# Three late score tiles exponentiated by VectorE, and the last chunk's tables made in two halves

## The chip, the cores and the metric

The kernel runs on one NeuronCore of a Trainium2 chip. The metric is the device time of one execution in microseconds (us), as the median of several. TensorE (PE in the profile) does matmuls, ScalarE (ACT) activations, VectorE (DVE) elementwise work, GpSimd (POOL) and SyncE (SP) mostly issue transfers here.

## The reference

Two mixers read the same input x (2048 positions, 448 channels, bf16) and are blended by a gate per position.

```
g = sigmoid((x * gate_w).sum(-1))
a = attention(x): 16 heads of 28 channels, one shared key/value head
    p = softmax(q k^T / sqrt(28)) ; o = p v ; a = o wo
b = state space convolution along positions:
    K[d,l] = Re( sum_n C[d,n] exp(dt[d] A[d,n] l) dt[d] B[d,n] ),  n < 256
    y[:,d] = causal convolution of x[:,d] with K[:,d] (by FFT of twice the length) ; b = y + x * Dskip
out = g * a + (1 - g) * b
```

The attention has 16 x 2048 x 2048 scores, all of which need an exponential. The convolution kernel K has 448 x 2048 entries, each a sum over 256 complex modes.

## The kernel before

**Attention.** The scores are cut into 1024 tiles of 128 keys by 512 queries. Sixteen blocks of queries and heads (index `i`) each hold 64 tiles: 16 key tiles for four heads. Tiles are worked in sets of three and two alternately (`sets` in `main`). For each set TensorE writes the scores to PSUM banks 0 to 4 (`qk`, lines 483, 1504 and 1498), ScalarE takes the exponential of the whole set in one instruction (line 1546) into `expT`, a ring of 15 tiles in SBUF, and two sets later TensorE multiplies four tiles at a time by the values (`pv`, lines 1570 and 1564) into the bank `psB`. The softmax sum is a column of ones among the values. When a block of 64 is done, `norm` copies `psB` out, sends the sums through DRAM and scales the result (lines 1237 to 1249); `outp` multiplies by the output matrix. The last block is finished in three parts (`PARTS`, `scaled`, `last`), so that little is left behind the last exponential. `early` adds two of the four head groups' products for the last block beforehand; `HELD` names the convolution steps behind which that is put.

**Convolution.** The channels are worked in 14 chunks of 32 (`c`). For each, `masters` squares the modes' step repeatedly and writes bf16 copies to `mbf` (line 1015), and `tables` (lines 1038 to 1088) builds on VectorE the powers from which K is made: five levels of complex products, each twice as wide as the one before it (lines 1052 and 1067), a real decay table in `tmp` (1071, 1075), and its products (1081, 1085, 1088). Two small copies on POOL start a chunk's tables. `kgen` turns them into K by matmuls (line 1111), in two halves of 16 channels with 32 matmuls each, stages them in `kstg` (1123), and stores them to DRAM (`KP`). `tload` reads them back as shifted tiles in `T` or `U`, and `conv` multiplies these with the input (1178), scales by 1 - g (1188), folds the result (1199) and adds it to the output tile `O` (1208). Chunk c has convolutions 2c and 2c + 1; the last chunk, `LASTQ` = 13, has 26 and 27. All tables of a chunk are made before any of its `kgen` matmuls.

**Order.** Every operation is entered with its reads, writes, an estimated length and a priority. `Prog.schedule` then plays all engines forward by these estimates and writes down a fixed order for each; dependences between engines become semaphore waits. Where TensorE would be idle, it puts in a filler matmul (line 1453). Its constants (`PUSH`, `SLACK`, `LATE` among others) say how much later than estimated a transfer or an operand may be taken to arrive. `HOLDC` holds two convolution steps of chunk 12 behind the last `kgen`. At run time each engine works through its own list strictly in order.

**Buffers of the change.** `xT` holds the input for the query projections, `qM` a wide copy of the queries, used by those score tiles that run on the full array (line 1504); late sets (`ROWS` = 320 and on) don't use it. Line 192 issues every transfer.

Of the kernel before, what the change touches and what calls it, by code (L numbers as in the profile page):

```python
# [7 lines left out]
ALU = mybir.AluOpType  # L8
# [4 lines left out]
P = 128  # L13
# [8 lines left out]
W2 = 2 * D  # L22
# [26 lines left out]
HELD = ((27, 3), (27, 9), (27, 15), (27, 21))  # L49
# [11 lines left out]
HOLDC = (((24, 8), 7), ((25, 0), 7))  # L61
# [19 lines left out]
        120, 165, 138, 131, 139, 152, 140, 167, 164, 154, 188, 168, 189, 169, 193, 190, 191, 195, 1739, 197,  # L81
        1740, 198, 200, 1741, 202
# [36 lines left out]
class Prog:  # L119
# [13 lines left out]
    PUSH, PUSHES = 1.1, 100.0  # L133
    POOL = (7, 5)
    SLACK = {"pe": 500.0, "dve": 300.0}
    FAR = 2500.0
    LAZY = {1.15: 200.0, 1.55: 200.0, 1.58: 200.0, 1.6: 200.0}
    LATE = 1000.0
# [362 lines left out]
class Kernel:  # L501
# [442 lines left out]
    def qproj(self, i):  # L944
# [30 lines left out]
        if True:  # L975
            pg.dma([(self.qM.v(32 * h, 32, s * XQ + 512 * h, [[1, 512]]), self.qT.v(32 * h, 32, 512 * s, [[1, 512]]))
                    for h in range(4)], (128, 1024), f"qm{s}", rd=[("q", s)], wr=[("qM", s)], pr=0, eng="pool", extra=4500)

    def masters(self, b):
# [13 lines left out]
        for k in range(11):  # L993
# [7 lines left out]
            if k == 5:  # L1001
# [13 lines left out]
            pg.op("dve", lambda e, off=off: e.tensor_copy(mbf.v(0, P, off, [[128, 2], [MC, nb], [1, 64]]),  # L1015
                                                          self.seedz.v(0, P, o, [[W2, 2], [64, nb], [1, 64]])),
                  el(2 * n, 1.92), rd=[kr, ki] + first + done, wr=[("mb", k)], pr=pr)

    def tables(self, c):
# [24 lines left out]
        for lv in range(5):  # L1044
# [25 lines left out]
        rk = [("tmp", 0), ("tmp", 1)]  # L1070
        vo(lambda e: e.tensor_copy(rho.v(0, P, 62, [[64, 32], [1, 2]]), mq(0)), 64,
           [("mq", 0)], rk)
        for lv in range(5):
            w = 1 << lv
            vo(lambda e, w=w, lv=lv: e.tensor_tensor(rho.v(0, P, (32 - 2 * w) * 2, [[64, 32], [2, w], [1, 2]]),  # L1075
                                                     rho.v(0, P, (32 - w) * 2, [[64, 32], [2, w], [1, 2]]),
                                                     self.mq.v(0, P, lv * W2 + 64 * c, [[2, 32], [0, w], [1, 2]]), ALU.mult), w * 64,
               [("mq", lv)] + rk, rk)
# [11 lines left out]

    def kgen(self, c):
# [4 lines left out]
        keys = self.tabkeys  # L1096
        ko = self.kstg
        rs = ko.rs
        for q in range(2):
            G = self.grp()  # L1100
            for k in range(4):
                m = 4 * q + k

                def mm(e, m=m, k=k, G=G):
                    for comp in range(2):
                        for half in range(2):
                            cg = half * 16 + 2 * m
                            for u in range(2):
                                fo = lo + comp * PL + (32 + cg) * 64 + u
                                mo = FM + comp * FP + cg * 64 + u  # L1110
                                r = e.matmul(
                                    G.v(64 * u, 64, 128 * k, [[1, 128]]),
                                    tab.v(0, P, lo + comp * PL + cg * 64 + u, [[2, 64]]),
                                    tab.v(0, P, fo, [[64, 2], [mo - fo, 2], [2, 32]]),
                                    start=(comp == 0 and half == 0), stop=(comp == 1 and half == 1),
                                    tile_position=(0, 64 * u), skip_group_check=True)
                    return r
                o = pg.op("pe", mm, 245, mode="h", ni=16, rd=keys,
# [298 lines left out]
    def main(self):  # L1417
        pg = self.pg
        kT, qT, expT, vaug = self.kT, self.qT, self.expT, self.vaug
        NTL = 1024  # L1420
        sets, t = [], 0
        while t < NTL:
            n = min(2 if len(sets) % 2 else 3, NTL - t)
            sets.append(list(range(t, t + n)))
            t += n
# [14 lines left out]
        for ts in sets:  # L1440
            bs, es = sorted(t % 5 for t in ts), sorted(t % RING for t in ts)
            for t, b, x in zip(ts, bs, es):
                bank[t], ring[t] = b, x
        spread = lambda x, n: [[512 * (x[1] - x[0]), n], [1, 512]] if n > 1 else [[1, 512]]
# [13 lines left out]
        def qk(s):  # L1458
# [4 lines left out]
            def row(e):  # L1463
                r = None
                if ts[-1] >= NLAST:
# [41 lines left out]
            if s < 8 or len(ts) == 3 or s >= 14 and (ts[0] % 64 < NEWQ or s >= ROWS):  # L1507
# [7 lines left out]
                if ts[-1] < NLAST and ts[0] > 64:  # L1515
                    o.pre = pre
# [23 lines left out]
            es = [ring[t] for t in ts]  # L1540
            ew = [("e", x) for x in es]
            for t in ts:
                x = ring[t] if t <= RING else 0
                ew += ["Wk"] if x == RING - 1 else ["Wv", "Wvg", "Wm"] if x == RING - 2 else self.xk(3) if 9 <= x < 13 else self.xk(2) if 5 <= x < 9 else []
            n = len(ts)
            o = pg.op("act", lambda e: e.activation(expT.v(0, P, 512 * es[0], spread(es, n)),  # L1546
                                                self.psS.v(0, P, 512 * bs[0], spread(bs, n)),
                                                AF.Exp, scale=SQ), 63.5 + 426.5 * n, rd=bk, wr=ew, pr=0)
            self.lastexp = o.i
            if s == GATEOUT:  # L1550
                self.gw.deps[o.i] = 1

        def pv(v):
# [4 lines left out]
            def mm(e, ts=ts):  # L1558
                if ts[0] >= NLAST:
                    q0, nq = PARTS[declast(ts[0])[0]]  # L1560
                    for x in range(512 // nq):
                        for t in ts:
                            p, kt, h = declast(t)
                            r = e.matmul(self.psB.v(32 * h, 32, q0, [[1, nq]]), vaug.v(0, P, 32 * (kt + x), [[1, 32]]),
                                         expT.v(0, P, 512 * ring[t] + nq * x, [[1, nq]]),
                                         start=(kt + x == 0), stop=(kt + x == 15), tile_position=(0, 32 * h), skip_group_check=True)
                    return r
                for t in ts:
                    i, kt, h = dec(t)
                    r = e.matmul(self.psB.v(32 * h, 32, 0, [[1, 512]]), vaug.v(0, P, 32 * kt, [[1, 32]]),  # L1570
                                 expT.v(0, P, 512 * ring[t], [[1, 512]]),
# [7 lines left out]
            o = pg.op("pe", mm, 230, rd=["va"] + [("e", ring[t]) for t in ts], wr=[("b", 6)], pr=0.5 if v < NTL // 4 - 2 else -1, mode="c", ni=8)  # L1579
# [6 lines left out]
            if end:  # L1586
# [4 lines left out]
                self.copied = o.i  # L1591
        nv = 0
        self.lastpv = None
        self.pvs, self.qks = [], []
        for s in range(len(sets)):
            qk(s)
            last = sets[s][-1]
            if s >= 2:
                while nv < NTL // 4 and 4 * nv + 3 <= sets[s - 2][-1]:
                    pv(nv)  # L1600
# [12 lines left out]
        for b, (c0, nb) in enumerate(BLOCKS):  # L1613
            self.masters(b)
            for c in range(c0, c0 + nb):
                self.tables(c)
# [59 lines left out]
```

## Time and profile before

| | |
|---|---|
| median of 3 runs | 497.94 us (495.91 to 501.37) |
| profiled execution | 499.41 us |
| its span | 497.5 us |
| TensorE busy | 468.4 us, 94% of the span |
| VectorE busy | 456.5 us, 92% |
| ScalarE busy | 482.7 us, 97% |
| exponentials (line 1546) | 464.8 us in 410 instructions |
| mean granted TensorE clock | 0.993 |

Durations are of one profiled execution. "Busy" merges overlapping instructions; the length of one instruction can overlap the next one's start on the same engine, so the distance from start to start is what an instruction occupies. Idle time ahead of an instruction is printed with what ended it; "issue" means that the profile shows nothing that it waited for. A matmul group's "x18" counts instructions. The granted clock is TensorE's share of full speed.

### The profile page before, as it was taken

How to read it: one execution, taken by the hardware profiler on the slowest of the kernel's cores; microseconds unless marked ns; L12 is line 12 of the kernel's file. 1: busy time of each engine (PE TensorE's matmuls, PEld its weight loads, DVE VectorE, ACT ScalarE, POOL GpSimd, SP SyncE). 2: the span in 40 equal slices, each digit the busy share in tenths (PEclk: the TensorE clock that was granted, in tenths of full speed). 3: DMA queues.
4: the chain of work that ended last, by engine and by line, in shares of the span. 5: the costliest groups of instructions: out<-in, count | busy, mean ns of one | idle time of the engine just before them, and what ended most of it. 6: DMA issues, size and time to landing. Idle time of an engine off the chain costs nothing.

```text
span 497.5 us, 17528 instructions
## 1 busy us (share of the span) xinstructions
PE 468.4 (94%) x7685; PEld 219.8 (44%) x7752; DVE 456.5 (92%) x850; ACT 482.7 (97%) x434; POOL 213.9 (43%) x390
## 2 busy tenths in 40 slices
PE   8999999999999999999999999999999999989997
PEld 6433233452542534454443335444435444444554
DVE  6999999999999999999999999999999999993325
ACT  6999999999999999999999999999999999998995
POOL 8402135334143434749339355872747342521110
PEclk9999999999999999999999999999999999997999
DMA  8970015818408654896914919886494949492842
GB/s 244 278 155 13 3 33 147 276 28 267 134 18 260 196 156 117 239 267 177 289 30 95 324 25 255 243 217 172 114 241 108 290 84 356 141 327 89 241 153 71
DMA packets 91912, 85.45 MB, mean 172 GB/s; under 512 B 25242, under 2 KB 86860, under 8 KB 91836
## 3 DMA queue, kind: packets, MB, share of 16 engines
q1 hardware_dynamic: 80938, 72.54, 50.1%
q0 software_dynamic: 10624, 11.70, 10.1%
q8 instruction: 61, 1.00, 0.8%
q14 instruction: 15, 0.12, 0.1%
q10 hardware_dynamic: 274, 0.08, 0.1%
HBM read 76.36 MB, written 5.23 MB: 164 GB/s over the span
## 4 chain that ended last, share of the span: by engine, by line
ACT 41%; DVE 30%; PE 20%; DMA 4%; SPq 2%; issue 1%; ACTq 0%
ACT expT L1546 41%; DVE tab L1052 10%; DVE tab L1067 5%; PE psS L483 3%; PE psB L1570 3%; DVE tab L1081 2%; PE psX L1178 2%; PE psS L1178 2%; DMA T<-in_B_A_re_dram 2%; SPq L192 2%; PE psS L1504 2%; DVE tmp L1075 2%; DMA T<-KP_scratch 1%; DVE kstg L1123 1%; DVE msq L995 1%
## 5 line engine op out<-in xcount | busy, mean ns | idle before, releaser
L1546 ACT ACTIVATE expT<-psS 128x1536 bf16<-128x1536 f32 (+1 forms) x410 | 464.8, 1331 | 5.9 <-PE psS L483 4.7
L1052 DVE TENSOR_TENSOR tab<-tab,mbf 128x256 bf16<-128x256 bf16 (+4 forms) x140 | 138.7, 996 | 0.0
L483 PE MATMUL psS<-qT,kT 32*128 32x512 bf16 x703 | 100.8, 383 | 7.6 <-ACT expT L1546 3.6
L1570 PE MATMUL psB<-expT,vaug 128*32 128x512 bf16 x992 | 99.5, 391 | 0.9 <-DVE acc L1237 0.9
L192 POOL DMA_DIRECT2D KP_scratch<-kstg x104 | 57.8, 562 | 48.1 <-DVE kstg L1123 47.1
L1067 DVE TENSOR_TENSOR tab<-tab 128x256 bf16<-128x256 bf16 (+4 forms) x140 | 77.6, 575 | 0.0
L1504 PE MATMUL psS<-qM,kT 128*128 128x512 bf16 x183 | 59.6, 382 | 8.5 <-issue 5.8
L1570 PEld LDWEIGHTS psB<-expT,vaug 128*32 128x32 bf16 x992 | 25.5, 93 | 76.3 <-issue 72.4
L192 POOL DMA_DIRECT2D U<-in_A_x_dram x60 | 39.8, 667 | 37.7 <-PE psX L1199 13.1
L1453 PE MATMUL psB<-ident,one 128*128 128x512 bf16 x167 | 54.5, 393 | 0.0
L192 POOL DMA_DIRECT2D qM<-qT x64 | 33.1, 525 | 43.2 <-DVE denT L1243 14.8
L192 POOL DMA_DIRECT2D rdenB<-R_scratch x60 | 30.7, 518 | 37.4 <-DMA R_scratch<-denT 37.4
L1178 PE MATMUL psX<-T,U 128*26 128x128 bf16 (+3 forms) x1792 | 44.2, 227 | 1.2 <-issue 0.8
L1488 PEld LDWEIGHTS <-kT 32*128 32x128 bf16 x703 | 24.4, 91 | 46.3 <-issue 35.8
L1178 PEld LDWEIGHTS psX<-T,U 128*26 128x26 bf16 (+3 forms) x1792 | 37.1, 138 | 14.4 <-issue 9.8
L1178 PE MATMUL psS<-T,U 128*26 128x128 bf16 (+3 forms) x1600 | 36.7, 226 | 2.5 <-issue 1.9
L1178 PEld LDWEIGHTS psS<-T,U 128*26 128x26 bf16 (+3 forms) x1600 | 31.5, 138 | 13.4 <-issue 10.3
L1081 DVE TENSOR_TENSOR tab<-tab,tmp 128x1984 bf16<-128x1984 bf16 x28 | 32.5, 1181 | 0.1
L192 POOL DMA_DIRECT2D denT<-acc x15 | 10.7, 716 | 49.8 <-DVE acc L1237 47.7
L1075 DVE TENSOR_TENSOR tmp<-tmp,mq 128x64 bf16<-128x64 bf16 (+4 forms) x70 | 25.6, 365 | 0.3
L1453 PEld LDWEIGHTS psB<-ident,one 128*128 128x128 bf16 x167 | 14.4, 98 | 24.9 <-issue 17.1
L995 DVE TENSOR_TENSOR msq<-T 128x512 f32<-128x512 f32 (+1 forms) x40 | 24.8, 619 | 0.0
(201 smaller groups left out, 535.0 us busy)
## 6 DMA issues: line engine op xcount, KB each, us to landing
T<-KP_scratch SPq DMA_DIRECT2D x212, 272.0 KB, 5.4
rdenB<-R_scratch POOLq DMA_DIRECT2D x60, 64.0 KB, 3.9
U<-KP_scratch SPq DMA_DIRECT2D x12, 272.0 KB, 5.4
U<-in_A_x_dram SPq DMA_DIRECT2D x20, 112.0 KB, 3.2
qM<-qT POOLq DMA_DIRECT2D x64, 32.0 KB, 2.3
tab<-in_A_x_dram SPq DMA_DIRECT2D x4, 448.0 KB, 5.5
KP_scratch<-kstg POOLq DMA_DIRECT2D x104, 16.0 KB, 2.1
xT<-XS_scratch POOLq DMA_DIRECT2D x3, 448.0 KB, 4.9
```

The lines of the kernel that those rows point to most:

```text
L192: return [e.dma_start(o, i, **kw) for o, i in pairs]
L483: return e.add_instruction(mybir.InstMatmult(start_tensor_calc=True, stop_tensor_calc=True, tile_size=(32, 128), tile_position=pos, bass_s ...
L995: pg.op("dve", lambda e: e.tensor_tensor(m2(msq), z2, z2, ALU.mult), el(2 * n), rd=[kr, ki] + first, wr=["msq"], pr=pr)
L1052: mul = lambda e, o, a, b: e.tensor_tensor(o, a, b, ALU.mult)
L1067: vo(lambda e, dv=dv, tv=tv, k=k: e.tensor_tensor(dv, dv, tv, ALU.add if k else ALU.subtract), n, [kt[k], kd[k]], [kd[k]], 1.92 if lv else ...
L1075: vo(lambda e, w=w, lv=lv: e.tensor_tensor(rho.v(0, P, (32 - 2 * w) * 2, [[64, 32], [2, w], [1, 2]]), rho.v(0, P, (32 - w) * 2, [[64, 32], ...
L1081: vo(lambda e, k=k: e.tensor_tensor(tab.v(0, P, FM + k * FP + 2, [[64, 32], [2, 31], [1, 2]]), tab.v(0, P, lm + k * PL + 62, [[64, 32], [- ...
L1178: r = e.matmul(ps.v(32 * j, 32 - m0, 128 * k, [[1, 128]]), self.U.v(0, P, (4 * gi + j) % UA // UC * UW + (2 * m0 + par) * UC + (4 * gi + j ...
L1453: return e.matmul(t.v(0, P, off, [[1, 512]]), self.one.v(0, P, 2, [[0, P]]), self.ident.v(0, P, 0, [[0, 4], [1, P]]), start=b != 6, stop=b ...
L1504: return e.matmul(self.psS.v(0, P, 512 * b, [[1, 512]]), kT.v(0, P, 128 * kt, [[1, 128]]), self.qM.v(0, P, (i % 2) * XQ + 512 * h, [[1, 51 ...
L1546: o = pg.op("act", lambda e: e.activation(expT.v(0, P, 512 * es[0], spread(es, n)), self.psS.v(0, P, 512 * bs[0], spread(bs, n)), AF.Exp, ...
L1570: r = e.matmul(self.psB.v(32 * h, 32, 0, [[1, 512]]), vaug.v(0, P, 32 * kt, [[1, 32]]), expT.v(0, P, 512 * ring[t], [[1, 512]]), start=(kt ...
```

## The change

Three score tiles, numbers 956, 1007 and 1006, are taken out of ScalarE's sets and exponentiated by VectorE instead. In the order of score tiles they are moved forward to places 947, 967 and 982 (`DX`, `DXP`), so three sets of three hold one tile fewer for ScalarE. VectorE computes the exponential in eight fp32 steps over 128 x 512: scale by log2 e and clamp, round to an integer, take the fraction, build the power of two as int16 bits of a bf16 number, and multiply by a polynomial in three steps. Scratch is `qM`, the result goes to `xT`; `pv` reads a tile from there. Query copies into `qM` for blocks 13 to 15 are left out.

The tables of chunk 13 are made for 16 of its 32 channels and then for the other 16 (`halftables` in place of `tables`), each with its own keys, so that `kgen`'s first 32 matmuls depend on the first half alone. The copies of masters of the last block become two instructions each, one for chunk 13 in an arrangement by halves; the decay masters are rearranged in place by one POOL copy, and the two starting copies on POOL become four. `HOLDC` is emptied, `HELD` names other convolution steps, and three planner constants differ.

```
-HELD = ((27, 3), (27, 9), (27, 15), (27, 21))
+HELD = ((26, 8), (26, 24), (27, 4), (27, 16))
-HOLDC = (((24, 8), 7), ((25, 0), 7))
+DX = (956,1007,1006,)
+DXP = (947,967,982,)
+HOLDC = ()
-    PUSH, PUSHES = 1.1, 100.0
+    PUSH, PUSHES = 1.0, 100.0
-    SLACK = {"pe": 500.0, "dve": 300.0}
+    SLACK = {"pe": 500.0, "dve": 250.0}
-    LATE = 1000.0
+    LATE = 800.0
...
-        if True:
+        if i < 13:
             pg.dma([(self.qM.v(32 * h, 32, s * XQ + 512 * h, ...
...
+            nc = nb - (c0 + nb > LASTQ)
+            if nc < nb:
+                pg.op("dve", halves, el(128, 1.92), rd=[kr, ki], wr=[("mh", k), ("mb", k)], pr=pr)
...
+    def halftables(self):
+        pg.op("pool", lambda e: e.tensor_copy(mq.v(0, P, 0, ...), mq.v(0, P, 64 * c, ...)), 500, rd=mqk, wr=["mqh"], pr=pr)
+        for q in range(2):
+            pg.op("pool", ...)
+            pg.op("pool", ...)
+            for lv in range(5):
+                for k in range(2):
+                    vo(... mul ..., 2 * n, ...)
+                for k in range(2):
+                    vo(... ALU.add if k else ALU.subtract ..., n, ...)
+            if q == 0:
+                rhos()
+            for k in range(2):
+                vo(... mul ..., 992, ...)
+            vo(... copy of one ..., 64, ...)
+            vo(... multiply by -1.0 ..., F2, ...)
+            self.halfkeys.append([("lh", q, l) for l in range(1, 13)] + fk)
...
-                o = pg.op("pe", mm, 245, mode="h", ni=16, rd=keys,
+                o = pg.op("pe", mm, 245, mode="h", ni=16, rd=keys or self.halfkeys[q],
...
-                                                AF.Exp, scale=SQ), 63.5 + 426.5 * n, rd=bk, wr=ew, pr=0)
+                                                AF.Exp, scale=SQ), 63.5 + 426.5 * n, rd=[("b", b) for b in ab], wr=ew, pr=0)
+            for t in ts:
+                if t in DX:
+                    dx(t)
...
+        def dx(t):
+            pg.op("dve", lambda e: e.tensor_scalar(y, psS bank, SQ * LOG2E, QK - 127.0, ALU.mult, ALU.max), el(512), ..., pr=-1)
+            do(lambda e: e.tensor_scalar(z, y, -QK, QMAG + 127.0, ALU.add, ALU.add), ky, kz)
+            do(lambda e: e.scalar_tensor_tensor(y, z, QMAG + 127.0, y, ALU.subtract, ALU.subtract), ky + kz, ky)
+            do(lambda e: e.tensor_scalar(sc, z, QMAG, 128.0, ALU.subtract, ALU.mult), kz, ...)
+            do(lambda e: e.scalar_tensor_tensor(u, y, QA[0], y, ALU.add, ALU.mult), ky, ku)
+            do(lambda e: e.scalar_tensor_tensor(z, u, QA[2], y, ALU.add, ALU.add), ky + ku, kz)
+            do(lambda e: e.scalar_tensor_tensor(u, u, QA[1], z, ALU.add, ALU.mult), ku + kz, ku)
+            do(lambda e: e.scalar_tensor_tensor(out, u, QA[3], out, ALU.add, ALU.mult), ku + dk, dk)
```

In the built kernels ScalarE's exponentials go from 205 of three tiles and 204 of two to 202 and 207 (one of a single tile in both). VectorE has 58 instructions more, POOL 12 transfers and two small copies fewer and five small copies more. SP's queue holds the store of the first half of chunk 13, then four tile loads into `U` and four into `T`, then the store of the second half, then eight tile loads; before, both stores came ahead of all of them. TensorE's and VectorE's orders agree with the old ones only at the beginning.

165 lines of the change are left out of this document (137 added, 28 removed).

## The prediction

> **What bounds the kernel now.** I read the busy totals first, then ScalarE's instructions in order of time with the gaps before them, then TensorE's over the widest gap, then VectorE's up to the last table. The profiled execution took 499.41 us with a span of 497.5 us, so 1.9 us lie outside the span; the median of the runs shown is 497.94 us, 1.5 us below it.
>
> ```profile
> PE 468.4 (94%) x7685; PEld 219.8 (44%) x7752; DVE 456.5 (92%) x850; ACT 482.7 (97%) x434; POOL 213.9 (43%) x390
> ```
>
> Three engines are nearly full, so the totals alone don't say which of them ends last. ScalarE's timeline (start, length, group, and in brackets the idle time ahead of it and what ended it) does:
>
> ```profile
> 21.22 77.20 ACT L1546 ACTIVATE expT<-psS 128x1536 bf16<-128x1536 f32 x68
> 98.91 31.79 ACT L1546 ACTIVATE expT<-psS 128x1536 bf16<-128x1536 f32 x28 [0.49 <-PE psS L483]
> ...
> 414.06 31.80 ACT L1546 ACTIVATE expT<-psS 128x1536 bf16<-128x1536 f32 x28 [0.38 <-PE psS L483]
> 446.80 2.47 ACT L1546 ACTIVATE expT<-psS 128x1536 bf16<-128x1536 f32 x2 [0.94 <-PE psS L483]
> 450.11 2.37 ACT L1546 ACTIVATE expT<-psS 128x1536 bf16<-128x1536 f32 x2 [0.84 <-PE psS L483]
> 453.55 38.33 ACT L1546 ACTIVATE expT<-psS 128x1536 bf16<-128x1536 f32 x34 [1.08 <-PE psS L483]
> 493.57 0.27 ACT L1309 ACTIVATE acc<-psB 32x128 f32<-32x128 f32 x1 [1.69 <-PE psB L1564]
> ```
>
> From 21.22 us to 491.88 us (453.55 + 38.33) ScalarE does nothing but exponentials. What isn't exponentials there is 5.9 us:
>
> ```profile
> L1546 ACT ACTIVATE expT<-psS 128x1536 bf16<-128x1536 f32 x205 | 316.2, 1542 | 4.9 <-PE psS L483 4.7
> L1546 ACT ACTIVATE expT<-psS 128x1024 bf16<-128x1024 f32 x204 | 229.0, 1123 | 1.0 <-PE psS L1504 0.9
> ```
>
> So the time is 21.2 us of start, the exponentials, 5.9 us of waiting and 5.6 us of ending (497.5 less 491.88). Of the waiting, 0.94 + 0.84 + 1.08 = 2.86 us lie in one place, between 445.9 and 453.6 us; about 3.0 us are spread over six other places. The one place is explained by TensorE's timeline and by two-microsecond windows (window; busy us of PE, PEld, DVE, ACT and POOL with counts; granted clock; DMA share; GB/s):
>
> ```profile
> 444.32 0.45 PE L1178 MATMUL psS<-T,U 128*30 128x128 bf16 x18
> 446.12 0.32 PE L1178 MATMUL psS<-T,U 128*26 128x128 bf16 x6 [1.35 <-issue]
> ...
> 451.08 1.89 PE L1453 MATMUL psB<-ident,one 128*128 128x512 bf16 x4
> ```
>
> ```profile
> 444.00:446.00 2.00, 0.76 (x24) 0.47 (x23) 1.97 (x4) 1.86 (x2) 0.26 (x1) 1.00 1.08 356
> 446.00:448.00 2.00, 1.89 (x23) 0.78 (x22) 0.97 (x1) 1.20 (x1) 0.00 (x0) 0.67 1.11 371
> 448.00:450.00 2.00, 2.00 (x17) 0.53 (x15) 1.39 (x2) 1.26 (x2) 1.04 (x3) 0.50 0.97 320
> 450.00:452.00 2.00, 2.00 (x12) 0.57 (x10) 1.05 (x3) 1.89 (x2) 1.22 (x2) 0.50 0.43 133
> 452.00:454.00 2.00, 2.00 (x18) 0.50 (x18) 0.00 (x0) 0.92 (x2) 0.00 (x0) 0.62 0.07 21
> ```
>
> TensorE stood for 1.35 us in the middle of a convolution with no releaser that the profile shows, under transfers at full share, and then ran at half its clock for some 7 us; score tiles came late and ScalarE waited three times. [...]
>
> **The change, part by part.**
>
> *Exponentials.* The three tiles leave three sets of three, which become sets of two: 205 and 204 instructions of the two widths become 202 and 207 in the built order. That is 3 x (1542 - 1123) ns = 1.26 us less on ScalarE, in the stretch after 453.55 us where it never waits. TensorE must keep up with that. In that stretch it is full too:
>
> ```profile
> 453.79 0.66 PE L1111 MATMUL psX<-tab 128*64 128x128 bf16 x16
> 454.38 0.39 PE L483 MATMUL psS<-qT,kT 32*128 32x512 bf16 x2
> ...
> 459.05 1.04 PE L1178 MATMUL psS<-T,U 128*32 128x128 bf16 x56
> 460.02 0.39 PE L483 MATMUL psS<-qT,kT 32*128 32x512 bf16 x3
> ```
>
> From start to next start, sixteen kernel-table matmuls (L1111) take 0.59 us, 0.037 each, and 56 convolution matmuls (L1178) take 0.97 us, 0.017 each. Counting both instruction orders behind the 943rd score tile, the kernel before has 480 convolution and 64 table matmuls there, the changed one 396 and 32: 84 x 0.017 + 32 x 0.037 = 2.6 us of TensorE's work moves ahead of that tile. So TensorE has 1.3 us more room than ScalarE gained, and I take the whole 1.26 us. If TensorE's order bound here regardless, it would be nothing.
>
> *Where that work goes.* Between tiles 880 and 943 the order loses seven of nine idle fillers and gains the same 2.6 us of real matmuls. These are covered only while ScalarE is behind TensorE; the fillers were the spare room of that stretch. It costs nothing if no gap like the one at 444.8 comes, and up to 2.86 us if one does.
>
> *The tables in halves.* VectorE is busy without a break until the tables' end. Its timeline:
>
> ```profile
> 405.08 1.22 DVE L1052 TENSOR_TENSOR tab<-tab,mbf 128x2048 bf16<-128x2048 bf16 x1
> 406.22 0.42 DVE L1075 TENSOR_TENSOR tmp<-tmp,mq 128x512 bf16<-128x512 bf16 x1
> ...
> 410.52 2.28 DVE L1052 TENSOR_TENSOR tab<-tab,mbf 128x4096 bf16<-128x4096 bf16 x1
> 412.72 0.68 DVE L960 TENSOR_REDUCE qT<-psS 128x512 bf16<-128x512 f32 x1
> 413.32 0.23 DVE L1243 RECIPROCAL denT<-denT 128x16 f32<-128x16 f32 x1
> ...
> 448.61 0.42 DVE L1208 TENSOR_TENSOR O<-O,psX 128x256 bf16<-128x256 bf16 x1 [1.64 <-PE psX L1199]
> ...
> 450.43 0.69 DVE L1088 TENSOR_SCALAR tab<-tab 128x2048 bf16<-128x2048 bf16 x1
> 455.73 0.69 DVE L1123 CAST kstg<-psX 128x512 bf16<-128x512 f32 x1 [4.61 <-PE psX L1111]
> ```
>
> A step of 4096 elements takes 2.20 us to the next start, one of 2048 takes 1.14, so a split step costs 2 x 1.14 - 2.20 = 0.08 us more. There are 24 more table steps and 10 more copies of masters: 34 x 0.08 = 2.7 us. Bounds: 0 (if the overlap hides it) and 34 x 0.23 = 7.8 us (a small instruction's whole length, from the reciprocal row); I take 2.7, the nearest like step. Without the 1.64 us stall the tables now end at 451.1 - 1.6 = 449.5 us. In the new order the second half's last step has ahead of it one more each of staging, scaling and output fold (0.60 + 0.60 + 0.33 us) and five of the first tile's eight steps, so it ends at about 449.5 + 2.7 + 1.5 + 2.5 = 456.2 us. Behind the first half's last step stand 8.2 us of table steps, those 1.5 and 2.5 us, so the first half ends near 444.0 us.
>
> Where TensorE meets them is told by score sets, counted along its timeline (they end with tiles 928, 953 and 960):
>
> ```profile
> 443.01 0.39 PE L483 MATMUL psS<-qT,kT 32*128 32x512 bf16 x3
> ...
> 457.73 0.39 PE L483 MATMUL psS<-qT,kT 32*128 32x512 bf16 x3
> ...
> 460.97 0.39 PE L483 MATMUL psS<-qT,kT 32*128 32x512 bf16 x2
> ```
>
> It meets the first half behind tile 928, scored from 443.0 us, and behind 16 small matmuls of the previous fold: about 444.0 us, so **there is no slack**, nor yet a loss. It meets the second half behind tile 960, scored by 461.3 us; less 2.86 and a tile's 0.42 that is 458.0, and 1.8 us remain. Everything behind it on TensorE, score tiles included, is held if it waits.
>
> *The eight steps.* fp32 rows for a scalar step and a two-tensor step:
>
> ```profile
> L886 DVE TENSOR_SCALAR T<-T x1: 629/629/629, 11.6 to 11.6; 128x896 f32<-128x896 f32 x1
> L887 DVE SCALAR_TENSOR_TENSOR T<-T x1: 1093/1093/1093, 12.3 to 12.3; 128x896 f32<-128x896 f32 x1
> ```
>
> By elements, 512 take about 0.36 and 0.62 us; six of the long kind (one reads PSUM) and two of the short give 4.4 us a tile, 13.3 us for three. VectorE waits 4.61 us ahead of the first staging copy and has more room after it, so this is hidden. With all at the long rate it is 14.9 us. The first tile's last three steps follow the second half's end, so it is done near 458.0 us; TensorE reads it behind tile 965, two sets (2 x 1.1 us) after 458.0. Its PSUM bank is free once its first step has run, 3.2 us of listed steps ahead of 456.2, near 453.0 us; the set that ends with tile 953 wants it, at 457.73 - 2.86 = 454.9 us. Neither decides.
>
> *Queues.* Twelve copies into the wide query tile go from POOL's queue, which idles there; nothing late hangs on them, so zero. SP stores each half's kernel apart and queues the second store ahead of only the last eight tile loads, which need it: zero, or if the half is late, its lateness, counted in the rival below. Five small POOL copies replace two: zero.
>
> *Planner constants.* They reorder TensorE from about its 565th instruction on. No row prices this; its bounds are the 3.0 us of scattered waits, lost or doubled, and I take zero, the middle, since nothing shows which sign it has.
>
> **Sum:** 499.41 - 1.26 - 2.86 = 495.29 us against the profiled execution. The lowest run shown, 495.91, is 3.5 us below the profiled one, much like an execution without the 2.86 us, so the median may hold only part of that: 497.94 - 1.26 - 2.86 = 493.8 to 497.94 - 1.26 = 496.7. I take **495.2 us**. A measurement of this kernel can tell about 1% (5 us) from no change.
>
> **Rivals.**
> Two windows of 5 us, one that ends in the gap and one later, are needed for the first:
>
> ```profile
> 440.00:445.00 5.00, 4.76 (x152) 3.01 (x145) 5.00 (x7) 5.00 (x6) 1.20 (x3) 1.00 1.01 316
> 470.00:475.00 5.00, 5.00 (x150) 2.97 (x152) 0.76 (x3) 5.00 (x5) 0.56 (x1) 1.00 1.05 352
> ```
>
> *The gap comes again*, here or in the denser stretch ahead of tile 943. For it: 152 matmuls and 145 loads in the 5 us that end in the gap, under full transfers, and the new order is denser. Against: 150 and 152 later, under the same transfers, had none. 499.41 - 1.26 = 498.15, by the median 496.7: about 497.6 us.
> *TensorE binds at the end*, so the exponentials' 1.26 us don't show: 499.41 - 2.86 = 496.55 us. For it: its rows there have no gaps; against: the 2.6 us moved away.
> *VectorE is late at tile 928* (slower). If the halves cost the upper 7.8 us instead of 2.7, the first half is ready some 3 us late (its share, 12 of 24 steps and all copies), TensorE stands for it, the score tiles stop, and the clock falls as it did. It decides once the wait passes the 1.35 us that was enough before. ScalarE loses about 2 us (3 less the set it has in hand) and 2.86 again: 495.29 + 2 + 2.86 = 500.2 us. [...]
> *More is gained*: the scattered 3.0 us go as well and the ending shortens as the last convolution comes five tiles sooner: 495.29 - 3.0 - 0.3 = 492.0 us.
>
> **How the numbers follow.** Forecast 0.45 (493.8 to 496.7), gap again 0.22, TensorE binds 0.10, VectorE late 0.11, more gained 0.12. The range runs from 491.5, just below the gaining case, to 500.2, the late case; it leaves out about 0.15. Faster by over 1% (below 493.0) takes most of the gaining case and a low tail of the forecast: 0.18. Slower by over 1% (above 502.9) needs the late case with a second loss: 0.05. The rest, 0.77, is within 1%.
>
> **What would show it.** Right: 202 and 207 exponentials; no granted clock below 0.9 past 440 us; no gap over 0.5 us ahead of an exponential behind tile 928; the first half's kernel matmuls starting near 444 us with no wait on VectorE, the second's near 458 us; scalar steps near 0.4 us and two-tensor ones near 0.65 us. Wrong: a wait on the tables ahead of the kernel matmuls followed by clock 0.5 (late), or a gap by issue elsewhere (gap again), or exponentials waiting on scores behind 455 us (TensorE binds).

## The result, and the profile after

Measured in turn on one chip, the changed kernel takes 493.26 us (median of 16; 492.31 to 495.50) against 495.45 us before (median of 16; 493.59 to 501.37). The ratio is 0.9965, with a 95% interval of 0.9949 to 0.9982: 2.2 us or 0.35% faster, clear of noise, and well inside the 1% at which the prediction drew its lines. The 497.94 us that the prediction started from was the median of three, and the profiled execution behind it, 499.41 us, was a long one; the new profiled execution took 493.01 us, with a span of 491.2 us.

ScalarE's timeline after (start, length, group, and idle time ahead with what ended it):

```profile
21.03 77.21 ACT L1654 ACTIVATE expT<-psS 128x1536 bf16<-128x1536 f32 x68
98.66 313.00 ACT L1654 ACTIVATE expT<-psS 128x1536 bf16<-128x1536 f32 x276 [0.42 <-PE psS L491]
412.02 36.27 ACT L1654 ACTIVATE expT<-psS 128x1536 bf16<-128x1536 f32 x32 [0.37 <-PE psS L491]
448.99 36.90 ACT L1654 ACTIVATE expT<-psS 128x1536 bf16<-128x1536 f32 x34 [0.70 <-PE psS L491]
487.51 0.27 ACT L1409 ACTIVATE acc<-psB 32x128 f32<-32x128 f32 x1 [1.62 <-PE psB L1696]
```

Exponentials run from 21.03 to 485.89 us (448.99 + 36.90), and the ending takes 5.3 us (491.2 less 485.89). Its groups by form (count, busy us and mean ns, idle time ahead):

```profile
L1654 ACT ACTIVATE expT<-psS 128x1536 bf16<-128x1536 f32 x202 | 310.1, 1535 | 1.7 <-PE psS L491 1.5
L1654 ACT ACTIVATE expT<-psS 128x1024 bf16<-128x1024 f32 x207 | 229.9, 1115 | 0.0
```

202 and 207 as forecast; waits are 1.7 us where the profile of before had 5.9. Between the two profiled executions the span falls by 6.3 us: 1.7 of it is the exponentials' busy time (464.8 to 463.1), 4.2 the waits, 0.3 the ending and 0.2 the start. Most of those 4.2 us belong to the one long execution of before, though: the medians differ by 2.2 us only.

The place where TensorE stood for 1.35 us has a successor. TensorE's timeline over it, and two windows (busy us of PE, PEld, DVE, ACT, POOL; granted clock; DMA share; GB/s):

```profile
446.62 0.50 PE L1278 MATMUL psX<-T,U 128*30 128x128 bf16 x19
448.08 0.55 PE L1278 MATMUL psX<-T,U 128*26 128x128 bf16 x21 [0.96 <-issue]
```

```profile
446.00:448.00 2.00, 1.12 (x45) 0.68 (x37) 2.00 (x2) 2.00 (x3) 1.58 (x4) 1.00 1.06 346
448.00:450.00 2.00, 1.92 (x54) 1.19 (x58) 1.89 (x4) 1.30 (x2) 0.00 (x0) 1.00 1.11 347
```

Again in the middle of a convolution, under transfers at full share and without a releaser, but for 0.96 us, and the clock stayed at 1.00. ScalarE lost 0.70 us.

The two halves meet TensorE thus. VectorE's last table step of each half, then TensorE's first kernel-table matmuls:

```profile
440.98 0.43 DVE L1182 TENSOR_SCALAR tab<-tab 128x1024 bf16<-128x1024 bf16 x1
...
454.68 0.42 DVE L1182 TENSOR_SCALAR tab<-tab 128x1024 bf16<-128x1024 bf16 x1
```

```profile
441.46 0.42 PE L1211 MATMUL psS<-tab 128*64 128x128 bf16 x8
...
455.94 1.11 PE L1211 MATMUL psX<-tab 128*64 128x128 bf16 x32
```

The first half ends at 441.41 us and its matmuls start 0.05 us later; the second ends at 455.10 us, 0.84 us ahead. VectorE's eight steps (duration ns min/median/max, first and last start, form):

```profile
L1674 DVE TENSOR_SCALAR qM<-psS x3: 684/684/691, 451.2 to 466.5; 128x512 f32<-128x512 f32 x3
L1677 DVE TENSOR_SCALAR qM<-qM x3: 415/417/418, 452.4 to 468.5; 128x512 f32<-128x512 f32 x3
L1678 DVE SCALAR_TENSOR_TENSOR qM<-qM x3: 691/691/693, 452.8 to 468.9; 128x512 f32<-128x512 f32 x3
```

The other five are 0.42 us (the int16 step) and 0.68 to 0.69 us each.

### The profile page after: what moved, and what is told of

Its sections match the earlier page's. It is cut to its first block, busy times and chain, and to the rows that moved or that the text cites. A ratio compares the mean times of both kernels' runs of the same rounds, so it can differ in the third digit from the quotient of the medians.

```text
span 491.2 us, 17558 instructions
## 1 busy us (share of the span) xinstructions
PE 464.4 (95%) x7675; PEld 220.7 (45%) x7744; DVE 472.0 (96%) x908; ACT 480.9 (98%) x434; POOL 213.3 (43%) x381
## 4 chain that ended last, share of the span: by engine, by line
DVE 46%; ACT 37%; PE 13%; issue 1%; DMA 1%; SPq 0%; ACTq 0%
ACT expT L1654 35%; DVE tab L1066 13%; DVE tab L1081 8%; DVE tab L1096 4%; PE psS L491 3%; DVE msq L1003 2%; DVE tmp L1090 2%; DVE cst L1288 2%; DVE kstg L1223 2%; PE psX L1278 2%; PE psB L1702 2%; DVE T L1005 1%; DVE T L1007 1%; DVE mbf L1024 1%; DMA U<-KP_scratch 1%
## 5 line engine op out<-in xcount | busy, mean ns | idle before, releaser
L1654 ACT ACTIVATE expT<-psS 128x1024 bf16<-128x1024 f32 (+1 forms) x410 | 463.1, 1321 | 1.7 <-PE psS L491 1.5
L1066 DVE TENSOR_TENSOR tab<-tab,mbf 128x256 bf16<-128x256 bf16 (+4 forms) x130 | 129.1, 996 | 0.0
L1702 PE MATMUL psB<-expT,vaug 128*32 128x512 bf16 x991 | 99.1, 390 | 0.7 <-DVE acc L1337 0.4
L1081 DVE TENSOR_TENSOR tab<-tab 128x128 bf16<-128x128 bf16 (+4 forms) x130 | 71.7, 571 | 0.0
L1702 PEld LDWEIGHTS psB<-expT,vaug 128*32 128x32 bf16 x991 | 25.4, 93 | 73.6 <-issue 70.5
L1559 PE MATMUL psB<-ident,one 128*128 128x512 bf16 x157 | 51.0, 384 | 0.0
L1278 PE MATMUL psX<-T,U 128*26 128x128 bf16 (+3 forms) x1856 | 46.3, 227 | 2.1 <-issue 1.5
L1278 PEld LDWEIGHTS psX<-T,U 128*26 128x26 bf16 (+3 forms) x1856 | 39.0, 138 | 16.9 <-issue 12.7
L200 POOL DMA_DIRECT2D qM<-qT x52 | 26.5, 518 | 31.8 <-DVE qT L974 15.5
L1278 PEld LDWEIGHTS psS<-T,U 128*26 128x26 bf16 (+3 forms) x1536 | 31.4, 138 | 13.3 <-issue 10.1
L1096 DVE TENSOR_TENSOR tab<-tab,tmp 128x1984 bf16<-128x1984 bf16 x26 | 29.9, 1179 | 0.1
L1211 PE MATMUL psS<-tab 128*64 128x128 bf16 x576 | 25.2, 223 | 0.8 <-DVE O L1308 0.4
L1090 DVE TENSOR_TENSOR tmp<-tmp,mq 128x64 bf16<-128x64 bf16 (+4 forms) x65 | 23.8, 365 | 0.2
```

The lines of the kernel that those rows point to most:

```text
L200: return [e.dma_start(o, i, **kw) for o, i in pairs]
L1066: mul = lambda e, o, a, b: e.tensor_tensor(o, a, b, ALU.mult)
L1081: vo(lambda e, dv=dv, tv=tv, k=k: e.tensor_tensor(dv, dv, tv, ALU.add if k else ALU.subtract), n, [kt[k], kd[k]], [kd[k]], 1.92 if lv else ...
L1096: vo(lambda e, k=k: e.tensor_tensor(tab.v(0, P, FM + k * FP + 2, [[64, 32], [2, 31], [1, 2]]), tab.v(0, P, lm + k * PL + 62, [[64, 32], [- ...
L1278: r = e.matmul(ps.v(32 * j, 32 - m0, 128 * k, [[1, 128]]), self.U.v(0, P, (4 * gi + j) % UA // UC * UW + (2 * m0 + par) * UC + (4 * gi + j ...
L1559: return e.matmul(t.v(0, P, off, [[1, 512]]), self.one.v(0, P, 2, [[0, P]]), self.ident.v(0, P, 0, [[0, 4], [1, P]]), start=b != 6, stop=b ...
```

## The experiments

Medians are of 6 to 16 executions; ratios are against the kernel before, measured in turn on the same chip in three batches of 29, 35 and 35 executions. The changed kernel was measured in the first comparison only, so a run and the changed kernel are compared through the kernel before: where their intervals overlap widely, a difference between them isn't shown. All runs but the two late ones and the one with short steps are planned anew, so that the order of every engine can differ besides the part that is named.

TensorE's mean granted clock is on record for these executions, and the table has it too. At a mean below 0.998 some 2 us of the span or more ran at half clock (0.002 x 493 us x 2; the clock records of the kernel before hold 1.00 and 0.50, nothing between). In the second and third batch every execution of the kernel before below 0.998 was slower than all others; in some other rows the two groups overlap (two steps: 493.49 us below, 495.61 us above).

| kernel | median us | ratio, 95% interval | executions below 0.998 | median of the others |
|---|---|---|---|---|
| before (three batches) | 495.27, 495.39, 495.18 | 1 | 7 of 29, 4 of 35, 6 of 35 | 495.13, 495.22, 494.94 |
| changed | 493.26 | 0.9965 (0.9949 to 0.9982) | 4 of 16 | 493.01 |
| tiles only, new constants | 497.17 | 1.0026 (1.0006 to 1.0046) | 7 of 12 | 496.66 |
| halves only, new constants | 494.24 | 0.9973 (0.9952 to 0.9993) | 0 of 12 | 494.24 |
| neither, new constants | 494.01 | 0.9973 (0.9956 to 0.9989) | 3 of 12 | 493.68 |
| changed, old constants | 500.82 | 1.0121 (1.0080 to 1.0162) | 5 of 6 | 500.06 (one) |
| first half 1.2 us late | 493.61 | 0.9956 (0.9934 to 0.9978) | 1 of 10 | 493.60 |
| first half 3 us late | 497.67 | 1.0032 (1.0008 to 1.0056) | 12 of 12 | none |
| two steps a tile | 494.18 | 0.9982 (0.9951 to 1.0012) | 6 of 12 | 492.78 |
| four tiles | 493.85 | 0.9965 (0.9939 to 0.9992) | 2 of 12 | 493.80 |
| short steps, same order | 494.40 | 0.9984 (0.9971 to 0.9997) | 4 of 12 | 493.75 |
| before, new constants | 496.75 | 1.0026 (1.0000 to 1.0052) | 8 of 12 | 494.45 |
| before, new holds | 495.19 | 0.9994 (0.9972 to 1.0017) | 1 of 12 | 495.15 |
| before, tiles | 496.06 | 1.0011 (0.9990 to 1.0032) | 4 of 12 | 495.43 |

**Which part pays.** Four runs take the parts apart within the changed kernel's constants.

```
-                self.tables(c) if c < LASTQ else self.halftables()
+                self.tables(c)
...
```

(The copies of masters and the reads of `kgen` go back to the old arrangement with it.)

> The changed kernel with the last chunk's tables made in one piece; tiles, constants and the rest stay. Theory (the 1.26 us off ScalarE is the main part of the gain of 2.2 us, 495.45 to 493.26): about 494.2 us. Rival (TensorE binds behind tile 943 unless the halves move 2.6 us of its work ahead, so the tiles alone give nothing): 495.4 us, with ScalarE waiting for scores behind tile 943. Rival (order and constants make the gain): 493.3 us.

Measured 497.17 us: worse than all three theories allowed. ScalarE's last rows of the profiled execution (span 493.0 us), and TensorE's behind the last score set:

```profile
450.36 33.98 ACT L1654 ACTIVATE expT<-psS 128x1024 bf16<-128x1024 f32 x31 [0.86 <-PE psS L491]
489.32 0.27 ACT L1409 ACTIVATE acc<-psB 32x128 f32<-32x128 f32 x1 [4.99 <-PE psB L1696]
```

```profile
483.00 0.39 PE L1604 MATMUL psS<-qT,kT 29*128 29x128 bf16 x4
...
484.44 0.51 PE L1278 MATMUL psS<-T,U 128*30 128x128 bf16 x20
485.75 0.45 PE L1299 MATMUL psS<-ident,cst 128*64 128x64 bf16 x16 [0.81 <-DVE cst L1288]
486.72 0.39 PE L1384 MATMUL psS<-msq,acc 128*128 128x4 f32 x2 [0.53 <-DVE O L1308]
```

ScalarE is done at 484.34 us, 1.5 us sooner than in the changed kernel, yet the ending takes 8.7 us instead of 5.3: 20 convolution matmuls and the fold of the last convolution stand behind the last scores, and TensorE waits there for VectorE's scaling (0.81 us) and its addition to the output tile (0.53 us) before it may finish the attention. So in this execution TensorE does bind without the halves, but not behind tile 943 with ScalarE waiting, as the rival had it: it binds behind the last exponential. That accounts for 1.8 us (spans of 493.0 and 491.2) of the 3.9 us between the medians: the profiled execution, 494.93 us, is the second fastest of the twelve, and of the slower ones no trace is kept. Seven of them had the clock below 0.998.

```
-DX = (956,1007,1006,)
-DXP = (947,967,982,)
+DX = ()
+DXP = ()
```

> The changed kernel with all three tiles back on ScalarE; the halves and constants stay. Theory: ScalarE is the bound, so moving TensorE's work ahead shows only as fewer waits, 0.5 us at most: about 495.0 us, exponentials 1.26 us more than in the changed kernel. Rival (the halves pay): 493.7 us. Rival (order and constants make the gain): 493.3 us.

Measured 494.24 us, between the theory and the rival. In its profile the exponentials end at 488.14 us of a span of 493.4, an ending of 5.3 us, as in the changed kernel. Against it the changed kernel has the three tiles, and is 0.98 us faster by the medians (1.23 us by those of undisturbed clock, 493.01 against 494.24). That is what 1.26 us off ScalarE would give, but the intervals of the two, 0.9949 to 0.9982 and 0.9952 to 0.9993, overlap almost wholly, so it isn't shown.

In this profile, too, TensorE stood in the middle of a convolution, for 1.41 us, and ScalarE lost 1.26 us; the granted clock stayed at 1.00 (windows as above):

```profile
448.81 0.56 PE L1278 MATMUL psX<-T,U 128*26 128x128 bf16 x21 [1.41 <-issue]
```

```profile
448.00:450.00 2.00, 1.19 (x40) 0.82 (x40) 1.60 (x3) 0.74 (x2) 0.00 (x0) 1.00 1.09 368
450.00:452.00 2.00, 2.00 (x77) 1.30 (x67) 1.76 (x3) 2.00 (x3) 0.00 (x0) 1.00 0.88 230
```

```
-DX = (956,1007,1006,)
-DXP = (947,967,982,)
+DX = ()
+DXP = ()
...
-                self.tables(c) if c < LASTQ else self.halftables()
+                self.tables(c)
...
```

> The changed kernel without tiles and without halves: what is left are the planner's constants, the emptied hold, the other places of the early products and the query copies left out. Theory: about 495.4 us, as the kernel before. Rival (order and constants make the gain): 493.3 us.

Measured 494.01 us, 1.3 us less than before, where the theory had no difference. So over half of the 2.2 us is there without tiles and halves. In this frame the tiles alone cost 3.2 us (497.17 against 494.01), and the intervals of these two are apart. The halves alone cost 0.2 us and both together gain 0.75; these differences are within the noise (0.9952 to 0.9993 and 0.9949 to 0.9982, against 0.9956 to 0.9989 here). So the study doesn't show that the tiles and halves together add to what the rest of the change gives; it shows that the tiles in an order like the one above cost time.

```
-    PUSH, PUSHES = 1.0, 100.0
+    PUSH, PUSHES = 1.1, 100.0
-    SLACK = {"pe": 500.0, "dve": 250.0}
+    SLACK = {"pe": 500.0, "dve": 300.0}
-    LATE = 800.0
+    LATE = 1000.0
```

> The changed kernel with the three planner constants of the kernel before (1.1, 300, 1000). Theory: the constants only move waits about, so 493.3 us within 0.7. Rival (the constants make the gain): 495 us or more.

Measured 500.82 us, 7.6 us above the changed kernel: the largest effect of the study, from three numbers that only the planner reads. ScalarE's last rows (span 499.6 us) and TensorE's from the last scores on:

```profile
487.96 1.94 ACT L1654 ACTIVATE expT<-psS 128x1536 bf16<-128x1536 f32 x2 [0.31 <-PE psS L1604]
495.11 0.27 ACT L1409 ACTIVATE acc<-psB 32x128 f32<-32x128 f32 x1 [5.22 <-PE psB L1696]
```

```profile
488.54 0.39 PE L1604 MATMUL psS<-qT,kT 29*128 29x128 bf16 x4
...
490.08 0.65 PE L1278 MATMUL psS<-T,U 128*32 128x128 bf16 x32
491.54 0.45 PE L1299 MATMUL psS<-ident,cst 128*64 128x64 bf16 x16 [0.82 <-DVE cst L1288]
492.51 0.39 PE L1384 MATMUL psS<-msq,acc 128*128 128x4 f32 x2 [0.53 <-DVE O L1308]
```

The same picture as with the tiles alone: 32 convolution matmuls and the fold come last, and the ending takes 9.7 us (499.6 less 489.90), 4.4 more than in the changed kernel. ScalarE also waits 2.7 us more in all (4.4 against 1.7 us by its groups).

This kernel has the halves, so they alone don't keep the ending short. What the traces have in common is where the last fold's matmuls stand. They come ahead of the last score tile in the changed kernel (481.06 against 484.35 us), with the halves only (480.79, 486.60), with neither (483.36, 485.00) and before (488.95, 490.41), and there the ending takes 5.3 to 5.6 us. They come behind it with the tiles only (485.75, 483.00), with the old constants (491.54, 488.54) and with the tiles in the kernel before (485.87, 485.55; its run is below), and there it takes 8.7, 9.7 and 6.7 us. TensorE in the changed kernel, then in the kernel before with tiles:

```profile
481.06 0.26 PE L1299 MATMUL psS<-ident,cst 128*64 128x64 bf16 x4
...
484.35 0.39 PE L1604 MATMUL psS<-qT,kT 29*128 29x128 bf16 x4
```

```profile
485.55 0.39 PE L1604 MATMUL psS<-qT,kT 29*128 29x128 bf16 x4 [0.24 <-ACT expT L1654]
485.87 0.45 PE L1299 MATMUL psX<-ident,cst 128*64 128x64 bf16 x16
```

**Where the 1.3 us without tiles and halves come from.** Two runs go from the other side, the kernel before.

```
-    PUSH, PUSHES = 1.1, 100.0
+    PUSH, PUSHES = 1.0, 100.0
-    SLACK = {"pe": 500.0, "dve": 300.0}
+    SLACK = {"pe": 500.0, "dve": 250.0}
-    LATE = 1000.0
+    LATE = 800.0
```

> The kernel before with the three new planner constants alone. The run with neither tiles nor halves gave 494.0 us against 495.3. Theory (the constants made that, by another order of TensorE from its 260th row on): 494.0 us. Rival (the emptied hold and the moved early products made it): 495.4 us.

Measured 496.75 us: slower, not faster. Its executions fall apart by clock: four at full clock have a median of 494.45 us, eight below 0.998 run from 495.56 to 499.56. The profiled one is of those, with the old trouble at the old place:

```profile
445.58 0.19 PE L1199 MATMUL psS<-ident,cst 128*64 128x64 bf16 x1 [1.65 <-issue]
```

```profile
446.00:448.00 2.00, 2.00 (x29) 0.71 (x29) 1.06 (x3) 1.56 (x2) 1.25 (x3) 0.52 0.93 298
448.00:450.00 2.00, 2.00 (x17) 0.34 (x9) 0.00 (x0) 1.08 (x2) 0.73 (x2) 0.50 0.68 147
```

```
-HELD = ((27, 3), (27, 9), (27, 15), (27, 21))
+HELD = ((26, 8), (26, 24), (27, 4), (27, 16))
-HOLDC = (((24, 8), 7), ((25, 0), 7))
+HOLDC = ()
```

> The kernel before with the emptied hold and the new places of the early products alone; TensorE's order differs from its 1800th row of 2033 on only. Theory (the constants made the 1.3 us): 495.4 us. Rival (these two did): 494.0 us.

Measured 495.19 us, no change. Neither the constants nor the holds alone make the 1.3 us; of what that run had besides, the query copies left out weren't tried by themselves, nor constants and holds together. The constants without a drop of the clock come nearest (494.45, four executions, against 494.9 to 495.2). What makes up these 1.3 us stays open.

```
+DX = (956,1007,1006,)
+DXP = (947,967,982,)
...
+            for t in ts:
+                if t in DX:
+                    dx(t)
...
```

> The kernel before with the three tiles on VectorE (and late query copies left out), its own constants and holds, tables in one piece. Its built order has the last fold's 16 matmuls behind the last score tile. Theory now (without the halves TensorE's last convolution comes too late, so that what ScalarE saves returns as a longer ending): 495.4 us or more, last exponential about 1.3 us sooner, ending 1 to 3 us longer than 5.6. First theory (1.26 us less on ScalarE show anyway): 494.1 us.

(The query copies for blocks 13 to 15 are left out in it too.) Measured 496.06 us, in the range of the later theory, and not to be told from no change (0.9990 to 1.0032). ScalarE's last rows (span 494.0 us):

```profile
476.20 11.13 ACT L1654 ACTIVATE expT<-psS 128x1536 bf16<-128x1536 f32 x10 [0.36 <-PE psS L1604]
490.31 0.27 ACT L1409 ACTIVATE acc<-psB 32x128 f32<-32x128 f32 x1 [2.98 <-PE psB L1696]
```

The exponentials end at 487.33 us and the ending takes 6.7 us, 1.1 more than before, so in a second order too what the tiles save comes back behind the last exponential.

**How late the first half may be.** Both runs keep every engine's order; only VectorE has reductions more that the planner doesn't know of, two in the first run and five in the second (range(5)).

```
-                vo(lambda e, k=k, fm=fm, lm=lm, q=q: mul(e, ...
+                def prod(e, k=k, fm=fm, lm=lm, q=q):
+                    if k == 1 and q == 0:
+                        for x in range(2):
+                            e.tensor_reduce(self.small.v(0, P, (4, 5, 6, 7, 13)[x], [[1, 1]]), self.kT.v(0, P, 0, [[1, 512]]), AX.X, ALU.max, apply_absolute_value=True)
+                    return mul(e, ...
+                vo(prod, 992, done + rk, [fk[k]], 1.92, pq)
```

> The changed kernel with two extra VectorE reductions of 512 elements (about 0.6 us each, results unused, unknown to the planner, so that every engine's order stays) ahead of the first half's last product: 1.2 us late. Theory (no slack at tile 928): TensorE waits about 1.2 us there, less than the 1.35 us that came before the slow clock, ScalarE loses 0.2 to 1 us: 493.5 to 494.3 us, clock 1.0. Rival (there is hidden slack): 493.3 us and no wait of the kernel-table matmuls on VectorE.

> As the run before with five extra reductions, 3.0 us late; all orders as in the changed kernel. Theory (the slower rival of the prediction): TensorE waits about 3 us at tile 928, ScalarE loses 2 us, and the clock falls to 0.5 for some 7 us and costs 2.9 more: 498.1 us, mean clock below 0.997. [...] Rival (hidden slack): 493.3 us.

Measured 493.61 and 497.67 us, both near what the theory had. In the second, TensorE's timeline at the place and the windows (span 496.0 us):

```profile
441.13 0.37 PE L491 MATMUL psS<-qT,kT 32*128 32x512 bf16 x3
443.95 0.45 PE L1303 MATMUL psX<-ident,cst 128*64 128x64 bf16 x16 [2.45 <-DVE cst L1292]
444.61 0.64 PE L1215 MATMUL psS<-tab 128*64 128x128 bf16 x8 [0.20 <-DVE tab L1186]
```

```profile
442.00:444.00 2.00, 0.04 (x2) 0.05 (x4) 2.00 (x8) 1.34 (x1) 0.00 (x0) 1.00 0.80 183
444.00:446.00 2.00, 1.80 (x30) 0.90 (x30) 1.97 (x9) 0.18 (x1) 0.56 (x1) 0.57 0.93 295
446.00:448.00 2.00, 2.00 (x27) 1.04 (x23) 1.93 (x5) 0.94 (x2) 0.00 (x0) 0.50 0.99 335
448.00:450.00 2.00, 2.00 (x38) 1.05 (x37) 0.98 (x3) 1.80 (x2) 0.84 (x2) 0.50 0.69 240
```

```profile
445.82 1.02 ACT L1658 ACTIVATE expT<-psS 128x1024 bf16<-128x1024 f32 x1 [2.49 <-PE psS L491]
447.91 1.45 ACT L1658 ACTIVATE expT<-psS 128x1536 bf16<-128x1536 f32 x1 [1.06 <-PE psS L491]
449.56 1.02 ACT L1658 ACTIVATE expT<-psS 128x1024 bf16<-128x1024 f32 x1 [0.20 <-PE psS L491]
451.53 39.16 ACT L1658 ACTIVATE expT<-psS 128x1536 bf16<-128x1536 f32 x36 [0.95 <-PE psS L491]
```

3.05 us of reductions make TensorE stand for 2.45 us, first at the fold, whose scaling stands behind the tables on VectorE, then at the tables themselves. ScalarE loses 2.49 us at once, and 1.06 + 0.20 + 0.95 = 2.2 us more while TensorE runs at half clock. The clock was below 0.998 in all twelve executions. The same place in the run with 1.2 us, from TensorE's timeline:

```profile
442.04 0.44 PE L1303 MATMUL psX<-ident,cst 128*64 128x64 bf16 x16 [0.69 <-DVE cst L1292]
```

TensorE stood for 0.69 us there and for 0.21 us at the tables right behind it, and the clock was below 0.998 in one execution of ten. By its time alone, 0.35 us above the changed kernel's, this run can't be told from hidden slack; the two waits on VectorE tell against slack. So a first lateness costs little, and one that stops TensorE for 2.45 us costs 4.4 us.

**Are the steps hidden?** The first run of this group leaves out the exponential of the three tiles but for its first step and a copy, which takes the place of the other seven steps:

```
-            do(lambda e: e.tensor_scalar(z, y, -QK, QMAG + 127.0, ALU.add, ALU.add), ky, kz)
...
-            do(lambda e: e.scalar_tensor_tensor(out, u, QA[3], out, ALU.add, ALU.mult), ku + dk, dk)
+            do(lambda e: e.tensor_scalar(out, y, 1.0, 1.0, ALU.mult, ALU.mult), ky, dk + ...
```

> The changed kernel with two of the eight steps for each of the three tiles: the first, which reads PSUM, and a copy to the result's place. It leaves out the rest of the exponential of three tiles. VectorE has 18 steps, about 10 us, less behind tile 947. Theory (the steps are hidden): 493.3 us within 0.7. Rival (the steps hold score tiles or value matmuls): 492.3 us or less.

Measured 494.18 us, but the planner made another order for it, whose ending is 3.8 us of waiting where the changed kernel has 1.62, and half of its executions had the clock drop. So it doesn't separate the steps from the order, and the next one keeps the order and narrows the data of the steps behind the first (the int16 step keeps its 512 columns):

```
+            yf, sf = z, sc
+            y, z, u, out, _ = (b.v(0, P, o, [[1, 32]]) for b, o in ...
...
-            do(lambda e: e.tensor_scalar(sc, z, QMAG, 128.0, ALU.subtract, ALU.mult), kz, ...
+            do(lambda e: e.tensor_scalar(sf, yf, QMAG, 128.0, ALU.subtract, ALU.mult), kz, ...
```

> The changed kernel with six of the eight steps of each tile narrowed to 32 of 512 columns (it leaves out the exponential of the other columns); every engine's order is that of the changed kernel, and VectorE has about 9 us less to do behind tile 947. Theory (the steps are hidden): 493.3 us within 0.7. Rival (the steps hold TensorE): 492.3 us or less.

Measured 494.40 us (493.75 at full clock), not less than the changed kernel's 493.26 with all of them, though six steps of each tile have 32 columns there instead of 512. So the steps hold up nothing that shows in the time. That it is 1.1 us more by the medians, with intervals that overlap, has no explanation here.

```
-DX = (956,1007,1006,)
-DXP = (947,967,982,)
+DX = (956, 1007, 1006, 1005)
+DXP = (947, 967, 982, 992)
```

> The changed kernel with a fourth tile, number 1005 at place 992, on VectorE. VectorE has some 6 us free behind 460 us. Theory (each tile takes 0.42 us off ScalarE as long as the steps are hidden): 492.8 us. Rival (its steps come too late and hold the last value matmuls): 494 us or more.

Measured 493.85 us with the same ratio as three tiles: between the two expectations, and not to be told from no change. In its profile (span 490.1 us) the exponentials end at 484.12 us, so the ending takes 6.0 us instead of 5.3: the 0.42 us come back there. No version of the study is shown to beat the changed kernel.

## Why the prediction was right or wrong

The direction and the range were right: 493.26 us in 491.5 to 500.2, within 1% of before. The range also held 495.45 us, no change at all. The point, 495.2, was 1.9 us high, mostly because it was set against a median of 497.94 that came out as 495.45 on more executions. Of the 2.7 us that it stood below that median, 2.2 were measured, and that this is close is partly luck: the 2.7 us were made of 1.26 us for the tiles and half of the stall of 2.86 us, while 1.3 of the 2.2 us measured are there without tiles and halves, in terms that the sum had at zero.

*Exponentials, 1.26 us, taken whole:* the instruction counts were right, the gain isn't shown. Against the halves only, the tiles come out 0.98 to 1.23 us faster, within the noise; without the halves, in two different orders, they show as nothing or as a loss. The step's condition, that TensorE must keep up, was the right one: where the last fold comes behind the last scores, what ScalarE saves is lost again. Its picture of "TensorE binds" was not: ScalarE isn't held in the last stretch, the loss appears behind the last exponential. And 2.6 us of work moved ahead of tile 943 don't settle it, since with the old constants the same tiles and halves end with the fold last.

*The stall of 2.86 us goes:* wrong as a gain of the change. Most executions of the kernel before have no fall of the clock: 17 of 99 had a mean below 0.998, against 4 of 16 of the changed kernel. The sum took a term from one long execution for a property of the kernel. The hint was in the times shown, and the step named it (the lowest run was 3.5 us below the profiled one) and dropped only half of the term.

*Planner constants, zero:* wrong in size. With tiles and halves the old constants cost 7.6 us, while in the kernel before the new ones alone bring no gain. The bounds, 3.0 us of scattered waits lost or doubled, looked at the waits alone; of the 8.4 us between the two profiled spans (499.6 and 491.2) 4.4 are in the ending, in which matmuls the order leaves behind the last scores. The new order's end was counted for the prediction (the last convolution comes five tiles sooner) and priced at 0.3 us; that is what the ending gave between the profiles, 5.6 to 5.3. The 1.3 us that are there with neither tiles nor halves come from something among constants, holds and query copies, all taken as zero; which of them stays open.

*Tables in halves:* the extra on VectorE was taken as 2.7 us and the first half's end as 444.0 us; it came at 441.41, and TensorE with it, so both were read some 2.6 us late. The conclusion, no slack and no loss, held (0.05 us), since both came early by the same amount. For the second half 1.8 us of slack were forecast and 0.84 measured.

*The eight steps:* 0.42 and 0.69 us where 0.36 and 0.62 were worked out by elements, since a part that doesn't shrink with the elements was scaled too (629 ns for 896, 417 for 512); 14.9 us in all instead of 13.3. Hidden, as forecast.

*The rival of a late VectorE:* it did not happen, and the run with 3 us shows that its price was about right: 4.4 us measured (497.67 against 493.26), 4.9 forecast. The fall of the clock that it counted on came too: the mean was below 0.998 in all twelve executions, and in the profiled one the clock was 0.50 behind the gap of 2.45 us (446 to 450 us).

*The gap comes again* happened in part: 0.96 us at 448.08 us in the profiled execution, without a fall of the clock there, while 4 of 16 executions had one. One of the signs of being right failed with it: ScalarE lost 0.70 us behind tile 928, where 0.5 was the limit.

## What to carry to other kernels

When several engines are full, taking work off the one that ends last pays only if the next one's last work is moved ahead as well: look at what its order leaves behind the last instruction of the first. A planner's constants can be worth more than the change that they were retuned for (7.6 us here, against 2.2 for the whole change), so a change in such a kernel is to be judged by runs of each part within the same constants, and even then each part brings an order of its own. A stall in one profile is to be checked against the spread of the times before it is booked as a gain.

## What the runs showed of the hardware

In three profiled executions TensorE's granted clock fell to 0.50 behind a gap: of 1.35 us (before, 446.12 us), 1.65 us (before with new constants, 445.58 us) and 2.45 us (first half 3 us late, 443.95 us). It stayed there for 6.8 us in the first of them (446.70 to 453.52 us in its clock record) and in the third (6.8 us by its windows from 444 to 452 us), and the second one's mean of 0.993 stands for some 6.9 us (0.007 x 496.0 us x 2). With the old constants a gap of 1.33 us ended at 251.43 us; the four value matmuls (L1702) of 253.66 and of 255.50 us took 0.62 us, those of 249.45 and of 258.20 us 0.40. That execution's mean was 0.996.

The clock did not fall behind 0.96 us (changed, 1.00 in the windows from 446 to 452 us), nor behind 1.41 us (halves only, 1.00 from 448 to 452 us). Behind 0.69 us (first half 1.2 us late) the value matmuls from 443.37 to 449.34 us (L1706) took 0.40 us, as ahead of the gap. The gap of 1.41 us is longer than that of 1.35 us, so the length of a gap alone doesn't decide; what does isn't shown. With two steps a tile the profiled execution had a mean of 0.989, and behind which gap its clock fell isn't shown either.

The DMA share was 1.08 in the windows with the gaps of 1.35 and 1.65 us (444 to 446 us). The slice of the page that holds the gap of 1.33 us (249.8 to 262.3 us) moved 23 GB/s; that is some 290 KB, an estimated 0.8 us of transfers at the 356 GB/s measured from 444 to 446 us in the kernel before, so they can't have filled that gap.

Executions with a mean clock below 0.998 are 2 to 3 us slower by the medians, their gaps included: 498.0 against 495.2 and 497.4 against 494.9 us for the kernel before (second and third batch), 495.1 against 493.0 for the changed one.

What opens the gaps that the profile ends with "issue" isn't shown. From 20 us on, TensorE's timeline of before has four of 0.5 us or more (0.58 us at 98.28, 0.55 at 130.48, 0.91 at 311.52 and 1.35 at 446.12 us), that of the changed kernel two (0.54 us at 98.02 and 0.96 at 448.08 us).
